# Attention outputs of the local heads: from a transposed product with moving probabilities to a row product with DMA transposes

## The chip, the core and the metric

The kernel runs on one core of one Trainium2 chip. The core has five engines that run side by side, each with its own queue of instructions taken in order: TensorE (PE, with its weight loads shown apart as PEld), VectorE (DVE), ScalarE (ACT), GpSimd (POOL) and SyncE (SP). SP issues DMAs and does no arithmetic. The metric is the device time of one execution in microseconds; lower is better.

## The reference

Two stages, float32 in and out.

```python
scores = scale * np.matmul(q, k.transpose(0, 1, 3, 2))        # (8, 8, 576, 576), head size 64
mask_local   = (rel >= 0) & (rel < 32)                        # heads 0 to 3
mask_strided = (rel >= 0) & (pos[None] % 32 == pos[:, None] % 32)   # heads 4 to 7
attn = softmax(np.where(masks, scores, -1e9))
attn_out = np.matmul(attn, v)
x = attn_out.transpose(0, 2, 1, 3).reshape(4608, 512)
out = (x @ w_a) * (x @ w_b) @ w_out                           # d_ff = 1536
```

`rel` is the query position minus the key position. A local head looks at the last 32 keys, a strided head at every 32nd key.

## The kernel before

**Stages.** The 4608 tokens are cut into nine FFN tiles of 512 tokens. A tile is 16 slots: slots 0 to 11 each compute one block of 128 of the 1536 hidden columns (`ffn_ab`: four matmuls of `wa_sb` and four of `wb_sb` against `xT`, L581, then the ACT copy L598 and the DVE product L601 or L603), and slots 12 to 15 compute the output of the tile (`ffn_y`, L768, for the tiles 0 and 1; `ffn_ys`, L686, for the others). A slot takes some 2 us. `xT` holds x transposed: 128 features on the partitions, four feature blocks `c` (two heads each), and room for four batches of 576 tokens. Tile b is the first that reads the tokens of batch b.

**Attention between the slots.** The attention of batch b is spread over the slots of tile b - 1. A batch is eight units u = 0 to 7: `c, half = u // 2, u % 2`. Units 0 to 3 are the local heads (c is 0 or 1, three blocks of 96 queries with windows of 128 keys), units 4 to 7 the strided heads. For each unit `S` makes the probabilities: score matmuls (L385), an ACT exponential into `p` (L393), a DVE mask (L403). One or two slots later `V` makes the outputs. The order is written out by hand: `LATER` puts V0, V1, V2, V3 of a batch after the slots 1, 3, 5, 7 of the tile and V4, V5, V6, V7 at 9, 11, 12.5 and 14, and `S0` of the next batch at -1, that is after slot 15. `STEPS` has the same for batches 1 and 2 at places of their own. After the steps of a slot come the entries of `at`, which hold loads, the DVE transposes `step_D` of the next batch's q and k, and the stores of the tile before. All engines take their instructions in this one order.

**Two forms of V.** Batches 0 and 1 use `V_p`, `V_r`, `V_n`: the probabilities are the weights and V with a column of ones moves through (L442, 65 columns), so that queries lie on the partitions and the row sum is one number per row; DVE takes a reciprocal (L450, of 96 x 6) and multiplies (L465, 96 x 384) into a tile `x` with queries on the partitions. `step_X` then transposes x on TensorE (L511) and copies it to `xT` on ACT (L523). Batches from `FIRST_D = 2` on use `step_VT`: V with 64 columns of ones is the weight and the probabilities move (L486, six matmuls of 96 columns for a local unit, eight of 72 for a strided one), so that the output is already transposed and the sums stand on the partitions 64 to 127. ACT takes the logarithm of the sums and the exponential of its negative (L495, L496) into a tile `r`, and two DVE products (L500 for local, L502 for strided units) write `xT`.

**Buffers.** `o`, the PSUM tile of V, has one buffer in this phase: the matmuls of a unit wait until the DVE products of the unit before have read it. The tile `x` of `V_n` (L458) and the tile `r` of `step_VT` (L488) have the same tag, `xr`, which has two buffers given in turn:

```python
x = sb.tile([128, RS * 4 * D], BF16, tag="xr", name="xr", bufs=2)                        # L458
r = sb.tile([128, RS * 4 * D], BF16, tag="xr", name="xr", bufs=2)[:64, :4 * W].bitcast(F32)  # L488
```

**SP's queue.** Each `step_D` ends in DMAs from SBUF to SBUF that SP issues (L342 two at a time for k, L346 four at a time for q). In the tile b - 1, where batch b's units run, the last part of b's own strided q is due at slot 1, which leads to ten DMAs in a row (qz four, kT two, qz four). From tile 2 on the stores of the tile before (`store_half`, L653, 512 KB each) are due at slots 2 and 3, from batch 3 on the last part of the local k of batch b + 1 at slot 5 (two DMAs) and that of its local q at slot 9 (ten more). For batch 3 itself, whose parts fall in tile 1, these two are due at slots 9 and 11 of that tile.

Of the kernel before, what the change touches and what calls it, by code (L numbers as in the profile page):

```python
# [14 lines left out]
FIRST_D = 2  # L15
# [6 lines left out]
LW = 96  # L22
# [8 lines left out]
def kernel(  # L31
# [10 lines left out]
    nc = tc.nc  # L42
    B, H, S, D = q.shape
# [114 lines left out]
    XR = 4  # L158
    xT = const.tile([128, KD, XR * S], BF16)
# [203 lines left out]
    def unit(u):  # L363

        c, half = u // 2, u % 2
        return (c, half, 128, LW, 3) if c < 2 else (c, half, NP, NP, 4)
# [46 lines left out]
    xn = {}  # L413

    def V_p(b, u):
        c, half, M, n, G = unit(u)
        p = ps.pop((b, u))
        if b == 0:

            o = psum4["o"].tile([128, 512], F32, tag="o", name="o")  # L420
            if c < 2:
                of = o[:, :2 * G * (D + 1)].rearrange("p (j g e) -> p j g e", j=2, e=D + 1)
                sm = of[:, :, :, D:]
            else:
                of = o.rearrange("p (j g e) -> p j g e", j=2, e=D)
                sm = psum4["sum"].tile([128, 2, 4, 1], F32, tag="sum", name="sum")
        else:
            o = psum4["o"].tile([128, 2, 512], F32, tag="o", name="o")
            of = o[:, :, :G * (D + 1)].rearrange("p j (g e) -> p j g e", e=D + 1)
            sm = of[:, :, :, D:]  # L430
        for i in range(G):
            for j in range(2):
                if c < 2:
                    vt = vl_buf[b % 2][:, (2 * c + j) * 6 + 3 * half + i, 0:D + 1]
                elif b == 0:
                    r = 2 * i + j
                    vt = nats[0, "v", c - 2][:NP, half, r * D:(r + 1) * D]
                else:
                    vt = vs_buf[b % 2][:, 2 * (c - 2) + half, 2 * i + j, 0:D + 1]
                w = vt.shape[1]  # L440
                pt = p[:M, j, i * n:i * n + 128]
                nc.tensor.matmul(of[:, j, i, :w], lhsT=pt, rhs=vt, start=True, stop=True)  # L442
                if b == 0 and c >= 2:
                    nc.tensor.matmul(sm[:, j, i], lhsT=pt, rhs=vl_buf[0][:M, 0, D:D + 1], start=True, stop=True)
        held[b, "o", u] = of[:n, :, :, :D], sm[:n]

    def V_r(b, u):
        c, half, M, n, G = unit(u)
        rc = sb.tile([128, 2, 4], F32, tag="rc", name="rc")
        nc.vector.reciprocal(rc[:n, :, :G].unsqueeze(3), held[b, "o", u][1])  # L450
        held[b, "rc", u] = rc

    def V_n(b, u):
        c, half, M, n, G = unit(u)
        ov, _ = held.pop((b, "o", u))
        rc = held.pop((b, "rc", u))
        if (b, c // 2) not in xn:
            x = sb.tile([128, RS * 4 * D], BF16, tag="xr", name="xr", bufs=2)  # L458
            xn[b, c // 2] = x[:n, :S // n * 4 * D].rearrange("p (g h d) -> p g h d", h=4, d=D)
        x = xn[b, c // 2][:, :, 2 * (c % 2):2 * (c % 2) + 2, :]  # L460
        if c < 2 or b >= FIRST_D:
            dst = x[:, G * half:G * half + G].rearrange("p g j d -> p j g d")
        else:
            dst = x[:, :, half, :].rearrange("p (g j) d -> p j g d", j=2)
        nc.vector.tensor_mul(dst, ov, rc[:n, :, :G].unsqueeze(3).to_broadcast([n, 2, G, D]))  # L465

    def step_V(b, u):
        if b >= FIRST_D:
            step_VT(b, u)
            return  # L470
        V_p(b, u)
        V_r(b, u)
        V_n(b, u)

    def step_VT(b, u):

        c, half, M, n, G = unit(u)
        p = ps.pop((b, u))
        o = psum4["o"].tile([128, 2, 512], F32, tag="o", name="o")
        for i in range(G):  # L480
            for j in range(2):
                if c < 2:
                    vt = vl_buf[b % 2][:, (2 * c + j) * 6 + 3 * half + i]
                else:
                    vt = vs_buf[b % 2][:, 2 * (c - 2) + j, 4 * half + i]
                nc.tensor.matmul(o[:, j, i * n:(i + 1) * n], lhsT=vt, rhs=p[:M, j, i * n:(i + 1) * n], start=True, stop=True)  # L486

        r = sb.tile([128, RS * 4 * D], BF16, tag="xr", name="xr", bufs=2)[:64, :4 * W].bitcast(F32)  # L488
        r = r.rearrange("p (j w) -> p j w", j=2)
        if c < 2:  # L490
            sums = o[64:, :, :W]
        else:

            sums, r = (t.rearrange(e, p=NP) for t, e in ((o[64:, :, :W], "d j (g p) -> d j p g"), (r, "d j (p g) -> d j p g")))
        nc.scalar.activation(r, sums, ACT.Ln)  # L495
        nc.scalar.activation(r, r, ACT.Exp, scale=-1.0)  # L496
        for j in range(2):
            dst = xT[64 * j:64 * j + 64, c, S * (b % XR):S * (b % XR + 1)]
            if c < 2:
                nc.vector.tensor_mul(dst[:, W * half:W * (half + 1)], o[:64, j, :W], r[:, j])  # L500
            else:
                nc.vector.tensor_mul(dst.rearrange("d (p r) -> d p r", r=RS)[:, :, G * half:G * (half + 1)],  # L502
                                     o[:64, j, :W].rearrange("d (g p) -> d p g", p=NP), r[:, j])
# [21 lines left out]
    def step_X(b, c):  # L525
# [20 lines left out]
    LATER = {-1: "S0", 0: "S1", 1: "V0", 2: "S2", 3: "V1", 4: "S3", 5: "V2", 6: "S4", 7: "V3", 8: "S5", 9: "V4", 10: "S6",  # L546
             11: "V5", 12: "S7", 12.5: "V6", 14: "V7"}
    FN = {"Tk": step_Tk, "Tq": step_Tq, "S": step_S, "V": step_V, "X": step_X, "W": lambda b, n: fast_w(n, slice(0, 3)),
          "s": S_px, "m": S_m, "L": lead_vl, "Pk": lambda b, c: pair_up("k", c), "Pq": lambda b, c: pair_up("q", c),
          "Z": lambda b, n: zero_qz(0, nc.vector, ((1, 1),)), "D": lambda b, n: step_D(FIRST_D, 0, "k", n)}  # L550
# [246 lines left out]
    with tc.manual_schedule(engines={ENG.PE, ENG.SP, ENG.Pool, ENG.DVE, ENG.Activation}):  # L797
# [11 lines left out]
        for x, src in ((raw[0], k), (raw[1], q)):  # L809
            nc.sync.dma_start(out=x[:96].rearrange("p (h r d) -> p h r d", h=2, d=D),  # L810
                              in_=src[0, 0:2].rearrange("h (p r) d -> p h r d", r=RL))
# [158 lines left out]
```

## Time and profile before

| what | value |
|---|---|
| time, median of 3 runs | 328.78 us (328.57 to 328.88) |
| span of the profiled execution, first to last instruction | 326.3 us |
| time of a run that lies outside such a span | 328.78 - 326.3 = 2.5 us |
| PE busy | 320.6 us, 98% of the span |
| DVE busy | 265.7 us, 81% |
| ACT busy | 202.7 us, 62% |
| POOL busy | 177.2 us, 54% |
| TensorE clock granted, mean | 0.999 |
| DMAs issued by SP for q and k (L342, L346), each | 0.59 us of SP's queue |

The profiled execution has a span and no time of its own; the 2.5 us are the difference between the median and that span. The tiles 1 to 6 take the stretches 57 to 92, 92 to 126, 126 to 160, 160 to 194, 194 to 228 and 228 to 262 us; batch b's units lie in tile b - 1.

How to read it: the page gives each engine's busy time, then the chain of work that ended last, then groups of instructions by source line with count, total, mean of one, and the idle time of the engine just before them with what ended it. The timeline gives single instructions with start and duration; a line with SPq is the issue of a DMA by SP, and its duration is how long SP's queue was held, not how long the data took.

### The profile page before, as it was taken

How to read it: one execution, taken by the hardware profiler on the slowest of the kernel's cores; microseconds unless marked ns; L12 is line 12 of the kernel's file. 1: busy time of each engine (PE TensorE's matmuls, PEld its weight loads, DVE VectorE, ACT ScalarE, POOL GpSimd, SP SyncE). 2: the span in 40 equal slices, each digit the busy share in tenths (PEclk: the TensorE clock that was granted, in tenths of full speed). 3: DMA queues.
4: the chain of work that ended last, by engine and by line, in shares of the span. 5: the costliest groups of instructions: out<-in, count | busy, mean ns of one | idle time of the engine just before them, and what ended most of it. 6: DMA issues, size and time to landing. Idle time of an engine off the chain costs nothing.

```text
span 326.3 us, 7676 instructions
## 1 busy us (share of the span) xinstructions
PE 320.6 (98%) x2820; PEld 205.5 (63%) x2820; DVE 265.7 (81%) x509; ACT 202.7 (62%) x329; POOL 177.2 (54%) x295
## 2 busy tenths in 40 slices
PE   8999999999999999999999999999999999999995
PEld 6754655455555587557999985569555954584474
DVE  6766888889778999999999999999877845647562
ACT  6764775478778765777677757875677643313321
POOL 8935839599966655875577557853312031232021
PEclk9999999999999999999999999999999999999999
DMA  9999999999999798799979999898033022004004
GB/s 151 154 204 201 204 184 182 173 171 136 132 213 116 95 97 79 77 217 125 83 72 199 138 86 77 160 180 84 20 77 115 2 67 64 0 2 129 1 2 129
DMA packets 98869, 37.50 MB, mean 115 GB/s; under 512 B 76688, under 2 KB 96016, under 8 KB 98832
## 3 DMA queue, kind: packets, MB, share of 16 engines
q0 software_dynamic: 85968, 19.48, 64.5%
q1 hardware_dynamic: 12576, 17.34, 18.4%
q8 instruction: 22, 0.36, 0.4%
q10 hardware_dynamic: 288, 0.20, 0.2%
q14 instruction: 15, 0.12, 0.1%
HBM read 39.51 MB, written 9.44 MB: 150 GB/s over the span
## 4 chain that ended last, share of the span: by engine, by line
PE 96%; DMA 2%; POOL 0%; DVE 0%; issue 0%; POOLq 0%; ACT 0%; DVEq 0%
PE mm L581 56%; PE mm L686 17%; PE mm L768 6%; PE st L385 5%; PE o L486 4%; DMA shared<-in_q_dram 2%; PE mm L714 2%; PE o L442 1%; PE ab L581 1%; PE misc L154 1%; PE tp L511 1%; PE tp L296 1%; PE end L714 1%; PE tp L287 0%; POOL shared L197 0%
## 5 line engine op out<-in xcount | busy, mean ns | idle before, releaser
L581 PE MATMUL mm<-xT,wa_sb 128*128 128x512 bf16 (+1 forms) x472 | 110.3, 357 | 0.0
L581 PE MATMUL mm<-xT,wb_sb 128*128 128x512 bf16 (+1 forms) x472 | 110.3, 357 | 0.0
L598 ACT COPY a_sb<-mm 128x512 f32<-128x512 f32 x106 | 62.1, 586 | 48.3 <-PE mm L581 47.6
L936 POOL CAST pace<-pf 1x1 f32<-1x1 bf16 x84 | 31.4, 374 | 84.0 <-DVE pf L601 80.7
L581 PEld LDWEIGHTS <-wb_sb 128*128 128x128 bf16 x480 | 46.3, 98 | 44.0 <-issue 0.2
L601 DVE TENSOR_TENSOR pf<-a_sb,mm 128x512 bf16<-128x512 f32 x84 | 56.4, 672 | 17.0 <-PE mm L581 13.8
L581 PEld LDWEIGHTS <-wa_sb 128*128 128x128 bf16 x480 | 42.7, 98 | 31.3
L393 ACT ACTIVATE p<-st 128x576 bf16<-128x576 f32 (+1 forms) x64 | 41.6, 650 | 11.7 <-PE st L385 11.1
L495 ACT ACTIVATE xr<-o 64x576 f32<-64x576 f32 x48 | 31.1, 649 | 25.0 <-PE o L486 24.2
L686 PEld LDWEIGHTS <-ps 128*128 128x128 bf16 x360 | 34.6, 98 | 3.9
L496 ACT ACTIVATE xr<-xr 64x576 f32<-64x576 f32 x48 | 32.9, 685 | 1.5
L500 DVE TENSOR_TENSOR xT<-o,xr 64x288 bf16<-64x288 f32 x48 | 21.5, 447 | 7.2 <-ACT xr L496 6.7
L502 DVE TENSOR_TENSOR xT<-o,xr 64x288 bf16<-64x288 f32 x48 | 21.5, 448 | 6.2 <-ACT xr L496 5.1
L686 PE MATMUL mm<-wf,ps 128*128 128x256 bf16 x216 | 26.4, 273 | 0.0
L768 PE MATMUL mm<-wo_sb,pf 128*128 128x512 bf16 x96 | 23.4, 379 | 0.0
L403 DVE TENSOR_TENSOR p<-p,mask_l 128x576 int16<-128x576 int16 x32 | 22.2, 694 | 1.2 <-ACT p L393 1.1
L243 POOL DMA_DIRECT2D vs<-in_v_dram x24 | 19.7, 821 | 3.0 <-PE st L385 2.2
L212 POOL DMA_DIRECT2D kl<-in_k_dram x24 | 16.1, 671 | 5.5 <-issue 3.6
L212 POOL DMA_DIRECT2D ql<-in_q_dram x24 | 16.0, 666 | 5.2 <-DMA wo_sb<-in_moe_w_out_dram 3.8
L603 DVE TENSOR_TENSOR pf<-a_sb,mm 128x512 bf16<-128x512 f32 x22 | 14.9, 676 | 4.3 <-ACT a_sb L598 2.8
L936 POOL COPY pace<-y_sb 1x1 f32<-1x1 f32 x16 | 2.8, 177 | 27.8 <-ACT y_sb L669 15.1
L686 PE MATMUL mm<-wf,pf 128*128 128x256 bf16 x144 | 17.6, 273 | 0.0
(162 smaller groups left out, 502.1 us busy)
## 6 DMA issues: line engine op xcount, KB each, us to landing
out_dram<-y_sb SPq DMA_DIRECT2D x12, 512.0 KB, 4.6
out_dram<-y_sb SPq DMA_DIRECT2D x10, 256.0 KB, 3.3
vl<-in_v_dram POOLq DMA_DIRECT2D x6, 384.0 KB, 6.8
kl<-in_k_dram POOLq DMA_DIRECT2D x24, 72.0 KB, 3.0
ql<-in_q_dram POOLq DMA_DIRECT2D x24, 72.0 KB, 3.0
vs<-in_v_dram POOLq DMA_DIRECT2D x24, 72.0 KB, 3.7
wo_sb<-in_moe_w_out_dram POOLq DMA_DIRECT2D x4, 384.0 KB, 9.2
natk<-in_k_dram POOLq DMA_DIRECT2D x20, 72.0 KB, 3.3
```

Of the source, the lines that this page charges most:

```text
L212: nc.gpsimd.dma_start(out=t[32 * h:32 * h + 32], in_=src[b, h].rearrange("(i y) d -> y i d", y=32))
L393: nc.scalar.activation(p[:M, :, :W], st[:M, :, :W], ACT.Exp, scale=scale)
L403: nc.vector.tensor_tensor(pi, pi, mk, op=ALU.bitwise_and)
L495: nc.scalar.activation(r, sums, ACT.Ln)
L496: nc.scalar.activation(r, r, ACT.Exp, scale=-1.0)
L500: nc.vector.tensor_mul(dst[:, W * half:W * (half + 1)], o[:64, j, :W], r[:, j])
L581: nc.tensor.matmul(ps_[:, c0:c0 + n], lhsT=w[:, kk, 128 * f:128 * (f + 1)], rhs=xT[:, kk, x0:x0 + n], start=(kk == first and c0 == 0), sto ...
L598: nc.scalar.copy(a_sb, ab[0])
L601: nc.vector.tensor_mul(pf[:, f, :].rearrange("p (i a s) -> p a i s", i=2, s=16), halves(a_sb), halves(ab[1]))
L686: nc.tensor.matmul(bank[b][:, q], lhsT=lhs(g, q), rhs=rhs(g), start=new and q == 0 and g == 0, stop=g == FG - 1, skip_group_check=True)
L768: nc.tensor.matmul(ybank[j], lhsT=pf[:, f, 128 * j:128 * (j + 1)], rhs=wo_sb[:, f], start=(f == 0), stop=(f == FD - 1))
L936: nc.gpsimd.tensor_copy(pace, done)
```

## The change

`step_V` sends the local units (c below 2) of batches 2 to 7 through `V_p`, `V_r` and `V_n`, as batches 0 and 1 do; strided units stay with `step_VT`. After the second half of each c, six DMA transposes, one per block of 96 queries, bring the block of x (96 queries x 128 features, bf16, 24 KB) into `xT`. SP issues them.

```diff
     def step_V(b, u):
-        if b >= FIRST_D:
+        c, half = u // 2, u % 2
+        if b >= FIRST_D and c >= 2:
             step_VT(b, u)
             return
         V_p(b, u)
         V_r(b, u)
         V_n(b, u)
+        if b >= FIRST_D and half == 1:
+            x = xn[b, 0]
+            for g in range(S // LW):
+                c0 = S * (b % XR) + LW * g
+                nc.sync.dma_start(out=xT[:, c, c0:c0 + LW],
+                                  in_=x[:, g, 2 * c:2 * c + 2].rearrange("p j d -> p (j d)"), transpose=True)
```

So each of six batches has four local units (24 in all) in the row form, and 12 DMA transposes (72 in all): six after V1 and six after V3. No instruction of the other units is changed, and no entry of the hand-written order.

## Prediction, made before the changed kernel was run

> **What bounds the kernel now.** I read the page's shares and its chain of work first.
>
> ```profile
> PE 320.6 (98%) x2820; PEld 205.5 (63%) x2820; DVE 265.7 (81%) x509; ACT 202.7 (62%) x329; POOL 177.2 (54%) x295
> PE 96%; DMA 2%; POOL 0%; DVE 0%; issue 0%; POOLq 0%; ACT 0%; DVEq 0%
> ```
>
> The chain is PE's for 96%. So only two things count: PE work that goes, and anything that makes PE wait. ACT and DVE work that goes is worth nothing by itself. Next the timeline around V5 of batch 5 (tile 4, a tile like most), all engines:
>
> ```profile
> 184.20 0.42 PE L486 MATMUL o<-p,vs 72*128 72x72 bf16 x8
> 184.66 0.65 ACT L495 ACTIVATE xr<-o 64x576 f32<-64x576 f32 x1 [0.55 <-PE o L486]
> 185.34 0.69 ACT L496 ACTIVATE xr<-xr 64x576 f32<-64x576 f32 x1
> 186.54 0.91 DVE L502 TENSOR_TENSOR xT<-o,xr 64x288 bf16<-64x288 f32 x2
> 188.22 0.43 PE L486 MATMUL o<-p,vs 72*128 72x72 bf16 x8
> ```
>
> V5's output leaves its only `o` buffer when L502 ends, at 187.45, and V6's matmuls take it at 188.22: 0.77 us of slack between an ACT instruction and PE. Then SP's queue in the same tile, the timeline of SP:
>
> ```profile
> 173.82 0.59 SPq L346 DMA_DIRECT2D qz10s<-tq  x1
> 174.45 0.60 SPq L346 DMA_DIRECT2D qz11s<-tq  x1
> 175.16 1.28 SPq L653 DMA_DIRECT2D out_dram<-y_sb  x2
> 176.55 3.33 SPq L342 DMA_DIRECT2D kT0l<-tk  x2
> 183.79 0.55 SPq L346 DMA_DIRECT2D qz00l<-tq  x1
> ```
>
> The reader is to see that SP is a real queue: a DMA from SBUF to SBUF holds it 0.59 us, and until 175.05 it is taken by ten of them whose first could start at 167.96. Behind two stores of 512 KB the next two took 3.33 us.
>
> **What the change does, part by part.**
>
> *PE, matmuls.* 24 units of six matmuls with 96 columns become six with 65. In the timeline a local unit of `step_VT` starts at 176.17 and the next matmul at 176.43: 0.26 us. A unit of L442 with 65 columns starts at 50.13 and its follower at 50.32: 0.19 us. 24 x 0.07 = 1.7 us less, on the path. That is all there is to gain.
>
> *ACT.* 24 x (649 + 685 ns) = 32 us go. Nobody waits for them now but the DVE products (ACT xr to DVE, 11.8 us of DVE idle in all), and DVE is not on the chain: 0.
>
> *DVE.* 24 x 2 x 447 ns = 21.5 us become 24 x (188 + 547 ns) = 17.6 us by the rows of L450 (96x6) and L465 (96x384). 3.9 us less, and V_n waits for PE alone, so `o` comes free earlier after a local unit. Hidden behind PE: 0.
>
> *PE, waits on DMAs.* `xT` now comes by 72 DMAs, so PE waits on DMA semaphores. A semaphore instruction at L486 takes 51 ns: 72 x 51 ns = 3.7 us at most, none if they pass while a matmul of 512 columns runs (eight take 1.73 us, 0.216 each). I take 0. The data itself has time: V3's transposes are due at slot 7 and the next tile reads at slot 16.
>
> *SP, 72 transposes.* The trace has none. SP is off the chain, so their cost lies in who waits for them. `x` and `r` share the tag `xr` with two buffers in turn: x of a batch takes one, r of V4 the other, and **r of V5 the one of x**. Its first writer is ACT's logarithm L495 of V5, and x is free only when the last of the 12 transposes has landed. Queued behind that logarithm on ACT are V5's exponential, the S7 exponential, the y copies; DVE's queue stands at L502; PE stands at V6, for `o`. The transposes of V3 in turn stand on SP behind everything due earlier. This wait is the heart of my forecast.
>
> *How long SP holds a transpose*, T, gap of 0.05 us included. Bounds: the shortest issue in SP's queue is 0.38 us (a store at 91.11), so 0.43; the longest SBUF-to-SBUF issue held behind stores is 2.13 us (143.97), so 2.18. I take **T = 0.9**: a plain DMA of this kind gives 0.64 and is the nearest row; the step up from it, for an operation of which no row tells, is my choice. Landing after issue: 1.8 to 3.7 us in these bursts, I take 3.0 (4.5 in tile 1, where the rows landed after 3.9 to 5.7).
>
> *Batch 5 worked out.* The burst of ten ends at 175.10. First store 0.7, six transposes 5.4, second store 0.7, the two of kT0l 1.3, the same hold behind the stores as now 2.1 (3.33 - 1.2), six transposes 5.4: SP ends at 190.7. The last was issued at 189.8 and lands at 192.8. V5's logarithm was at 184.66, so it starts 8.1 us late. Less the slack of 0.77, plus some 0.6 for V7 (L618, L403, L332, L616, L662 stand on DVE between V5's and V6's products, 3.3 us, and V7 follows V6 by 3.65 us with 0.2 us of slack): PE loses 7.9 us.
>
> *The other batches alike.* Batch 4: burst ends 140.57, hold 2.9, landed at 159.0, logarithm 150.40: 8.6 late, 8.5 lost. Batch 6: burst ends 208.56, hold 3.0, landed 227.1 against 218.69: 8.4 late, 8.3 lost. Batch 7: no local k behind the stores and loads over (DMA share 0.18 from 228 us on), so no hold and 2 us to land: 256.3 against 252.71, 3.6 late, 3.4 lost. Batch 3: burst ends 106.95, no such stores, 12 transposes and two kT: 121.1 against 116.37, 4.7 late, 4.6 lost. Batch 2: six transposes from 80.75 (behind kT1l), landed 89.8 against 85.04, 4.7 late, slack 0.34 there, 4.4 lost.
>
> Sum: 7.9 + 8.5 + 8.3 + 3.4 + 4.6 + 4.4 = **37.1 us lost**. Of the 1.7 us gained on PE I keep 0.4, what V0 saves (24 x 0.07 / 4): what comes later in a tile only lengthens the wait, since SP's burst sets when it ends. Net 36.7: the span goes from 326.3 to 363.0, and with the 2.5 us outside it, the time is **365.5 us**, against the median of 328.78.
>
> *What the unknowns move.* The sum changes by 11 T in five batches and 5 T in one, 60 us for each us of T. T = 0.43: 8.9 us, about 337. T = 0.64: 21.5 us, about 350. T = 2.18: 114 us, about 442. Each us of landing is worth 6 us, the hold behind the stores 8 us in all.
>
> *Two rules of the Trainium skill that stand against each other here.* "Advanced Engine Details and Errata", section "X-Bar Transpose (TRN2)", says that transposing DMAs are as fast as regular ones. "VectorE: DVE Perf Modes", section "The three transpose paths", gives 1309 ns for the DMA transpose of a 128 by 128 block against 390 ns on TensorE, and its table of rules sends a block to the DMA only where TensorE's PSUM output won't do, which speaks against this change. By the first the time would be about 350 us, as with the plain row of 0.64; by the second, read as 1.3 us of SP for each block, some 390 us. No run so far shows either.
>
> **The rivals.**
>
> *Faster: the transposes have landed when V5 asks.* Then only PE's 1.7 us remain: 327.1 us. This needs batch 5's last landing by 184.66 + 0.8. Without the transposes' own time the sum above reaches 179.9, plus 3.0 to land, and 11 T must fit in 2.6 us: T below 0.24, or a buffer of `xr` given otherwise than in turn. Against it: no issue in SP's queue is under 0.38. For it: landings near 1.8 us and no hold would allow 0.5. I give it 8%.
>
> *SP becomes the bound.* Now SP issues 24 DMAs and two stores in a tile of 34 us, 16.5 us. With T = 1.6 twelve more make 35.7: the local q of the next batch, due at slot 9 behind V3's transposes, comes late for S0 at slot 15 too. Time 37.1 + 60 x 0.7 = 79 us more, 408 us and up. For it: issues of 1.5 to 2.1 us behind stores. Against: most rows are at 0.59. 9%.
>
> *The DMA engines become the bound.* They are busy 95 to 98% in the stretches 92 to 228. Twelve transposes of 96 rows are 1152 packets a batch, at 39 ns (queue 0) to 76 ns (queue 1: 18.4% of 16 x 326.3 us over 12576 packets) over 16 engines 2.8 to 5.5 us. If the buffer wait is short and loads then miss their time, four tiles lose 11 to 22 us: 338 to 349 us. Against: DVE waited for a load 0.6 us in all. 7%.
>
> *Nothing to see*, the gain and a short wait cancelling: 2%.
>
> **How the numbers follow.** The buffer wait as worked out, with T between 0.43 and 1.6, has 74% and gives 336 to 410 us; its centre is my forecast, 365.5. The DMA rival lies inside. The range is 336 to 410; left out are the faster case, the cancelling one and the bound on SP, 19% together. Under 0.2% a measurement of this kernel can't be told from no change. Faster 0.08, within 0.2% 0.02, slower 0.90.
>
> **What would show it.** Right: ACT's L495 waits for the DMA `xT<-xr` six times, 3 to 9 us each, 38 us in all, at V5 alone; PE idles before L486 of V6, released by DVE L502; 72 DMAs of 24 KB on SP of some 0.85 us each; L495 and L496 fall to 24, L450 rises to 40; a local unit of L442 takes 0.19 us. Wrong: no wait of ACT on a DMA; waits of PE on the DMAs of `xT` at L581; DVE's V_n waiting for a transpose; idle PE at S0 instead of V6.

## The result, and the profile after

| what | before | after |
|---|---|---|
| time, median (lowest to highest) of 4 runs each | 328.83 us (328.57 to 328.94) | 396.98 us (396.13 to 399.35) |
| ratio, 95% interval | | 1.2064, 1.2 to 1.2128 |
| span of the profiled execution | 326.3 us | 394.5 us |
| PE busy | 320.6 us | 332.6 us, same 2820 matmuls |
| TensorE clock granted, mean | 0.999 | 0.922 |
| ACT busy | 202.7 us | 170.5 us |

The change makes the kernel slower by a fifth. The forecast was 365.5 us with a range of 336 to 410. Lines of the changed file stand 7 higher than before's from L474 on: the logarithm is now L502, the matmuls of the strided units L493, their products L509, the stores L660, the fast output L693. The transposes are issued at L479.

The page of the changed kernel: shares of the engines, the PE and clock rows of the 40 slices, the chain, and two groups.

```profile
PE 332.6 (84%) x2820; PEld 209.8 (53%) x2820; DVE 261.5 (66%) x509; ACT 170.5 (43%) x281; POOL 176.6 (45%) x295
PE   8999999991999399954999169990999739999995
PEclk9999999996899889995999869996799959999999
PE 69%; SPq 13%; DMA 6%; DVE 3%; ACT 3%; POOL 2%; issue 2%; POOLq 0%; ACTq 0%; DVEq 0%
L493 PE MATMUL o<-p,vs 72*128 72x72 bf16 x192 | 11.5, 209 | 55.5 <-DVE xT L509 55.5
L502 ACT ACTIVATE xr<-o 64x576 f32<-64x576 f32 x24 | 15.5, 647 | 74.5 <-DMA xT<-xr 55.8
```

The PE row has six holes, and the clock row has a dip at and after each. SP's queue, which was not in the chain before, has 13% of it, and the DMAs 6%. Of PE's 56.2 us of new idle time (394.5 - 332.6 against 326.3 - 320.6), 55.5 us stand ahead of one line, L493, and behind it stands a wait of ACT's logarithm on the DMA `xT<-xr`. The waits of that kernel (what waited, for what, us in all, times, longest):

```profile
PE o L493 <- DVE xT L509: 55.5, 6, 11.6
ACT xr L502 <- DMA xT<-xr: 55.8, 5, 13.4
ACT xr L502 <- DMA qz10l<-tq: 9.7, 1, 9.7
```

These are six waits of ACT, one in each of the batches 2 to 7: 9.75, 7.82, 11.06, 13.42, 12.87 and 10.58 us. One is put down to a q load; there too the logarithm began (95.05) 0.18 us after the last transpose had landed (94.87). The other five began 0.07 to 0.23 us after the last transpose of their batch. The timeline of tile 4 (V5 of batch 5) shows one of them; the last two lines come from its ACT and DVE queues, the first ones from PE's.

```profile
217.57 1.04 PE L693 MATMUL mm<-wf,ps 128*128 128x256 bf16 x8
230.21 0.64 PE L493 MATMUL o<-p,vs 72*128 72x72 bf16 x8 [11.61 <-DVE xT L509]
230.66 3.61 PE L693 MATMUL mm<-wf,ps 128*128 128x256 bf16 x16
...
227.76 0.65 ACT L502 ACTIVATE xr<-o 64x576 f32<-64x576 f32 x1 [13.42 <-DMA xT<-xr]
...
229.15 0.91 DVE L509 TENSOR_TENSOR xT<-o,xr 64x288 bf16<-64x288 f32 x2 [12.31 <-ACT xr L503]
```

ACT waits from 214.34 to 227.76, DVE's products follow, V6 on PE follows them. After that, sixteen matmuls of L693 take 3.61 us; in the kernel before sixteen of the same took 1.92:

```profile
188.48 1.92 PE L686 MATMUL mm<-wf,ps 128*128 128x256 bf16 x16
```

What the clock was can be read from busy times by stretch (length, busy us of PE, PEld, DVE, ACT and POOL, then granted clock, DMA share, GB/s):

```profile
218.60:223.90 5.30, 0.00 (x1) 0.00 (x0) 0.00 (x0) 0.00 (x0) 0.00 (x0) 1.00 0.73 82
223.90:230.20 6.30, 0.00 (x0) 0.02 (x1) 1.00 (x3) 2.38 (x4) 0.17 (x1) 0.50 0.15 35
230.20:234.10 3.90, 3.89 (x25) 2.92 (x26) 3.89 (x7) 1.41 (x3) 1.60 (x2) 0.50 0.81 101
234.10:238.70 4.60, 4.60 (x52) 4.14 (x51) 3.12 (x7) 2.50 (x4) 1.71 (x4) 1.00 0.24 22
```

The clock fell to 0.5 while PE stood, and stayed there for 3.9 us after PE had work again. The DMA engines were 73% busy in the first 5.3 us of the stall and 15% in the last 6.3, in which SP still issued transposes: there the queue that issues set the pace, not the transfers. SP's queue in the same tile:

```profile
204.38 0.59 SPq L346 DMA_DIRECT2D qz11s<-tq  x1
205.08 0.59 SPq L660 DMA_DIRECT2D out_dram<-y_sb  x1
205.71 9.41 SPq L479 DMA_TRANSPOSE xT<-xr  x6
215.23 0.59 SPq L660 DMA_DIRECT2D out_dram<-y_sb  x1
215.93 2.48 SPq L342 DMA_DIRECT2D kT0l<-tk  x2
218.46 8.08 SPq L479 DMA_TRANSPOSE xT<-xr  x6
226.66 0.56 SPq L346 DMA_DIRECT2D qz00l<-tq  x1
```

From the end of the burst of ten (204.97) to the end of the twelfth transpose (226.54) SP works without a gap. A transpose holds the queue 1.23 us (median of the 72), a plain DMA between SBUF places 0.59.

**Where the 68.2 us of span went.** 55.5 us are PE's six stalls (8.79, 6.01, 9.26, 11.61, 11.07, 8.78 us). 24.8 us of PE's busy time after them ran at half clock; half of that, 12.4 us, is my estimate of the loss. 1.8 us were gained: a local unit on PE takes 0.181 us where it took 0.255, 24 times. The sum is 66.1. Of the 2.1 us left, 0.95 arose before the change acts: the first output matmul of tile 0 started at 43.86 and not at 42.91. The rest is not assigned.

### The profile page after: what moved, and what is told of

Same layout as the page of the kernel before. It is cut to its first block, busy times and chain, and to the rows that moved or that the text cites. A ratio compares the mean times of both kernels' runs of the same rounds, so it can differ in the third digit from the quotient of the medians.

```text
span 394.5 us, 7706 instructions
## 1 busy us (share of the span) xinstructions
PE 332.6 (84%) x2820; PEld 209.8 (53%) x2820; DVE 261.5 (66%) x509; ACT 170.5 (43%) x281; POOL 176.6 (45%) x295
## 4 chain that ended last, share of the span: by engine, by line
PE 69%; SPq 13%; DMA 6%; DVE 3%; ACT 3%; POOL 2%; issue 2%; POOLq 0%; ACTq 0%; DVEq 0%
PE mm L588 42%; PE mm L693 13%; SPq L479 11%; PE mm L775 4%; DMA xT<-xr 3%; PE st L385 3%; SPq L342 2%; PE o L442 2%; PE o L493 2%; DMA vl<-in_v_dram 2%; DVE xT L509 2%; PE mm L721 1%; ACT xr L503 1%; ACT xr L502 1%; POOL shared L197 1%
## 5 line engine op out<-in xcount | busy, mean ns | idle before, releaser
L509 DVE TENSOR_TENSOR xT<-o,xr 64x288 bf16<-64x288 f32 x48 | 21.5, 448 | 77.5 <-ACT xr L503 77.1
L608 DVE TENSOR_TENSOR pf<-a_sb,mm 128x512 bf16<-128x512 f32 x84 | 56.5, 673 | 21.0 <-PE mm L588 17.6
L588 PEld LDWEIGHTS <-wa_sb 128*128 128x128 bf16 x480 | 42.3, 98 | 31.4
L493 PE MATMUL o<-p,vs 72*128 72x72 bf16 x192 | 11.5, 209 | 55.5 <-DVE xT L509 55.5
L502 ACT ACTIVATE xr<-o 64x576 f32<-64x576 f32 x24 | 15.5, 647 | 74.5 <-DMA xT<-xr 55.8
L693 PEld LDWEIGHTS <-ps 128*128 128x128 bf16 x360 | 39.4, 111 | 8.5
L493 PEld LDWEIGHTS <-vs 72*128 72x128 bf16 x192 | 10.0, 105 | 60.0 <-issue 57.2
L693 PE MATMUL mm<-wf,ps 128*128 128x256 bf16 x216 | 34.7, 326 | 0.0
L943 POOL COPY pace<-ya 1x1 f32<-1x1 f32 x6 | 2.0, 340 | 49.1 <-ACT ya L665 49.1
L465 DVE TENSOR_TENSOR xr<-o,rc 96x384 bf16<-96x384 f32 (+1 forms) x40 | 23.1, 579 | 1.3
L693 PE MATMUL mm<-wo_sb,ps 128*128 128x256 bf16 x144 | 18.7, 283 | 0.0
```

The costliest lines, as they stand in the source:

```text
L588: nc.tensor.matmul(ps_[:, c0:c0 + n], lhsT=w[:, kk, 128 * f:128 * (f + 1)], rhs=xT[:, kk, x0:x0 + n], start=(kk == first and c0 == 0), sto ...
L608: nc.vector.tensor_mul(pf[:, f, :].rearrange("p (i a s) -> p a i s", i=2, s=16), halves(a_sb), halves(ab[1]))
L693: nc.tensor.matmul(bank[b][:, q], lhsT=lhs(g, q), rhs=rhs(g), start=new and q == 0 and g == 0, stop=g == FG - 1, skip_group_check=True)
L943: nc.gpsimd.tensor_copy(pace, done)
```

## The experiments

Theory A, the prediction's: the tile `x`, which the transposes read, shares the tag `xr` with `r`, so V5's logarithm needs all twelve transposes landed, and SP's time for each of them sets when that is. Rival B: the stall has nothing to do with the buffer, and SP's time for the transposes would stop PE anyway, at S0, whose q loads queue behind them. A third question is whether SP's time goes by the instruction (A1) or by the block (A2).

### own: a buffer of its own for x

`x` of the batches from 2 on gets a tag of its own. The room for it comes from the V tiles of the local heads, cut from 128 to 80 columns a block, of which the row form reads 65.

```diff
+VL = 80
-    vl_buf = [const.tile([128, HL * 6, VW], BF16, name=f"vl{i}") for i in range(2)]
+    vl_buf = [const.tile([128, HL * 6, VL], BF16, name=f"vl{i}") for i in range(2)]
-            x = sb.tile([128, RS * 4 * D], BF16, tag="xr", name="xr", bufs=2)
+            x = sb.tile([128, RS * 4 * D], BF16, tag="xr", name="xr", bufs=2) if b < FIRST_D else sb.tile(
+                [128, RL * 4 * D], BF16, tag="xq", name="xq", bufs=1)
```

> The changed kernel with a buffer of its own for x (tag xq, one buffer), so that V5's r no longer waits for the transposes; the local V blocks take 80 columns instead of 128 to make room. Theory A (ACT's wait for x's buffer is the cause): the six waits of L495's counterpart on the DMA go, and with them the 55.5 us that PE stood before V6 and the 12 us of slower clock. But SP now needs 1.28 us for each transpose, so the local q of the next batch, behind V3's six, lands some 6 us after the place of S0 in the tiles 3, 4, 5 and some 3 us late in the tiles 1 and 2: PE idles at S0 instead, 25 us, time about 350 us (342 to 360). If SP has more room than that, 327 us. Theory B (SP or the DMA engines are the bound, whatever the buffer): 385 to 397 us, nearly unchanged.

Measured: 356.94 us (355.18 to 357.88), ratio to before 1.0839 (1.0778 to 1.0901); clock 0.971. ACT no longer waits for a DMA at the logarithm, and the 55.5 us at V6 are gone. PE's longest waits are now at the score matmuls:

```profile
PE st L386 <- DMA qz10l<-tq: 14.1, 3, 5.3
PE st L386 <- DMA qz00l<-tq: 4.5, 1, 4.5
```

SP's queue in tile 4 shows why:

```profile
203.87 7.79 SPq L481 DMA_TRANSPOSE xT<-xq  x6
211.77 0.67 SPq L347 DMA_DIRECT2D qz00l<-tq  x1
```

and PE's timeline has the wait:

```profile
215.25 0.20 PE L386 MATMUL st<-qz00l,kT0l 128*128 128x96 bf16 x1 [4.50 <-DMA qz00l<-tq]
```

The local q of the next batch, due at slot 9, is issued only from 211.77 on, behind V3's six transposes, and S0 stands 4.50 us for it, until 215.25. Five such stalls (tiles 1 to 5: 4.22, 1.1, 5.33, 4.5 and 4.57 us) make 19.7 us, and PE's busy time is 7.4 us above before's, at a clock that was 0.5 for 20.5 us. So the buffer is what the changed kernel waits for, and a buffer of its own is worth 396.98 - 356.94 = 40 us. Behind it stands the stall at S0 that B names, which the first one had hidden; with it the time is still 28 us above before's. Of B, only that stall is borne out: that the buffer has nothing to do with it, and the 385 to 397 us, are refuted.

### xr3: a third buffer for the shared tag

```diff
-            x = sb.tile([128, RS * 4 * D], BF16, tag="xr", name="xr", bufs=2)
+            x = sb.tile([128, RS * 4 * D], BF16, tag="xr", name="xr", bufs=3)
-        r = sb.tile([128, RS * 4 * D], BF16, tag="xr", name="xr", bufs=2)[:64, :4 * W].bitcast(F32)
+        r = sb.tile([128, RS * 4 * D], BF16, tag="xr", name="xr", bufs=3)[:64, :4 * W].bitcast(F32)
```

(with the same cut of the V tiles.)

> The changed kernel with three buffers for the tag xr instead of two (and local V blocks of 80 columns to make room). In turn, x's buffer then goes to r of V6 and not of V5, whose logarithm is due 4.0 us later (3.1 in tile 1). Theory A: each of the six waits moves from V5 to V6 and PE's from V6 to V7, and each gets some 4 us shorter: 55.5 us of PE idle become about 32, and with shorter idle times the clock drops less: 366 to 374 us. Theory B (SP's load itself): unchanged, 395 to 398 us.

Measured: 377.79 us (375.23 to 380.43), ratio 1.148 (1.1397 to 1.1562); clock 0.946. The waits, to be held against those of the changed kernel:

```profile
PE o L494 <- DVE xT L510: 37.5, 6, 8.3
ACT xr L503 <- DMA xT<-xr: 47.3, 6, 10.1
```

The same six waits are there, each one unit later: with three buffers in turn it is V6 that gets x's, and PE idles before V7. One unit more of time saves 18 us of the 55.5. The direction is A's; the size was missed, 37.5 us of idle PE where about 32 were expected, and the clock was 0.5 for 41.0 us, so that the time lies above the interval expected. The edit changes the buffers' turn and the width of the V tiles, and own has the same width without the wait: it is the turn that moved it by one unit.

### one: a single transpose for the six blocks of a pair of heads

`x` is laid out with the feature block c outermost, so that one DMA instruction can take all six blocks of 96 x 128; 12 instructions in place of 72. The buffers are the change's.

```diff
+                xn[b, 0] = x[:n, :RL * 4 * D].rearrange("p (c g j d) -> p g c j d", c=2, j=2, d=D)
...
-            for g in range(S // LW):
-                c0 = S * (b % XR) + LW * g
-                nc.sync.dma_start(out=xT[:, c, c0:c0 + LW],
-                                  in_=x[:, g, 2 * c:2 * c + 2].rearrange("p j d -> p (j d)"), transpose=True)
+            c0 = S * (b % XR)
+            nc.sync.dma_start(out=xT[:, c, c0:c0 + S].rearrange("p (g n) -> p g n", n=LW),
+                              in_=x[:, :, c].rearrange("p g j d -> p (g j d)"), transpose=True)
```

> The changed kernel with xr as it was (two buffers), but x laid out with c outermost, so that one DMA transpose brings all six blocks of a c (96 rows by 768 columns): 12 transposes in place of 72, the same bytes. Theory A1 (SP holds 1.23 us for each instruction, whatever its size): SP is free 6.4 us earlier after each group, V5 no longer waits: 327 to 332 us. Theory A2 (SP holds 0.2 us for each tile of 16 rows): one instruction holds it 7.4 us, the wait stays: 390 to 398 us. The rival that DMA engines bind: no gain either, but with short issues in SP's queue and long landings.

Measured: 339.21, 343.64 and 343.65 us (a fourth run, 346.31, does not enter the ratio), ratio 1.0374 (1.0264 to 1.0485). Neither number was met, but the question is answered: SP is held 1.20 to 1.45 us by an instruction of six blocks where no store stands directly ahead, as by one of a single block. SP's queue in tile 3 (batch 4):

```profile
139.46 0.61 SPq L662 DMA_DIRECT2D out_dram<-y_sb  x1
140.18 2.71 SPq L481 DMA_TRANSPOSE xT<-xr  x1
142.99 0.87 SPq L662 DMA_DIRECT2D out_dram<-y_sb  x1
143.96 3.02 SPq L342 DMA_DIRECT2D kT1l<-tk  x2
147.07 1.45 SPq L481 DMA_TRANSPOSE xT<-xr  x1
```

What A1 left out is what the stores ahead do: SP holds the first transpose and the two kT1l behind them longer (2.71 and 3.02 us), and the landing is late. The transpose issued at 147.07 landed 7.67 us later, behind two stores of 512 KB, and ACT's line of that tile reads

```profile
154.85 0.65 ACT L504 ACTIVATE xr<-o 64x576 f32<-64x576 f32 x1 [4.63 <-DMA qz11l<-tq]
```

(the load it names ended close by; the transpose landed at 154.75). Three long waits are left, in the batches 4, 5 and 6: 4.63, 6.05 and 5.18 us, with landings of 7.67, 6.33 and 5.13. PE idles 10.4 us for them, and the clock was 0.5 for 3.4 us around each, in 9.4 us of PE's busy time. The run of 339.21 us, whose mean clock was 0.999, suggests what that costs: it is 4.4 us shorter. These are the batches in which both stores of 512 KB and a load of local k stand ahead of the second transpose. Batches 2 and 3 have no such stores; batch 7 has them, but no local k, so that its second transpose was issued 4.4 us after the burst of ten ended (261.14 - 256.76) and not 7.7 (147.07 - 139.35). The batches 3 and 7 wait for no DMA; in batch 2 ACT waits 1.60 us (the transpose landed at 86.02, 5.06 us after its issue), which costs PE 0.65 us.

### own_one: both at once

> Both: x in a buffer of its own and one transpose for each c. Theory A1: nothing waits, PE's 1.7 us remain as the gain: 327 us. Theory A2: SP as full as with 72 transposes, PE idles at S0, about 350 us, as in the run with the own buffer alone.

Measured: 327.31 us (326.94 to 330.26, 10 runs) against 328.46, ratio 0.9967 (0.9938 to 0.9996); span 325.4. The page's first line is that of the kernel before, less 1.1 us:

```profile
PE 319.5 (98%) x2820; PEld 204.0 (63%) x2820; DVE 259.8 (80%) x509; ACT 171.0 (53%) x281; POOL 174.4 (54%) x295
```

No gap of PE above 0.8 us is left in the stretch of the change. With 12 instructions on SP and no compute instruction waiting for their landing, both mechanisms are gone, and what stays fits PE's shorter local units. The cut of the V tiles is in this kernel too; no run has it alone, so its part in the gain, if any, isn't told apart.

### tr_alone: the transposes alone, nobody waiting for them

The kernel before, with 72 transposes of a constant added where the change has them. They write a part of `xT` that is written again before it is read: work that the kernel doesn't need.

```diff
         if b >= FIRST_D:
             step_VT(b, u)
+            c, half = u // 2, u % 2
+            if c < 2 and half == 1:
+                for g in range(S // LW):
+                    c0 = S * ((b + 1) % XR) + LW * g
+                    nc.sync.dma_start(out=xT[:, c, c0:c0 + LW], in_=ident[:LW], transpose=True)
             return
```

> The kernel before, all units in its own form, with 72 DMA transposes of 96 x 128 added at the places of the change; they read the identity and write a part of xT that is written again before anyone reads it, so no unit waits for them. What is told apart: SP's time for the transposes by itself. Theory A: the local q of the next batch stands behind them on SP and PE idles at S0, as in the run with the own buffer (20 us of idle, 10 us of half clock); without that run's shorter local units about 358 us (350 to 362). If 72 transposes on SP cost nothing without the buffer wait: 328 to 330 us.

Measured: 363.94 us (359.08 to 364.04), ratio 1.1022 (1.0948 to 1.1096), a little above what was expected. Of the profiled run (364.04 us), 4.6 us were lost before the first added transpose (issued at 78.4): PE waited 1.60 us for a load of V at the start, its clock was 0.5 from 17.96 to 24.78, and the first output matmul came at 47.56 where before has 42.91. The waits:

```profile
PE st L385 <- DMA qz10l<-tq: 12.9, 3, 5.1
PE st L385 <- DMA qz00l<-tq: 7.9, 2, 5.0
```

The five stalls at S0 (20.8 us) stand in the same five tiles as own's (19.7 us). No data is waited for that a transpose brings, no buffer is shared: SP's queue time by itself costs some 30 us in this kernel (359.08 - 328.80 in the fastest run; 362.3 - 326.3 - 4.6 = 31.4 in the profiled one). This is the prediction's rival "SP becomes the bound", and it needs no buffer.

### one_late: the landing taken away instead of the shared buffer

As `one`, with the two stores of a tile moved behind V3's transpose.

```diff
-                do(16 * t + 18, store_half, 0)
+                do(16 * t + 24, store_half, 0)
...
-                do(16 * t + 19, store_half, 1)
+                do(16 * t + 25, store_half, 1)
```

> One transpose for each c and the two buffers of xr, as in the run that had 343.65 us, and the stores of a tile issued six slots later (slots 8 and 9 of the next tile), behind V3's transpose and not ahead of it. Theory: what is left of the wait there (three waits of ACT in the tiles 3 to 5, where the transpose landed 7.7 us after its issue behind two stores of 512 KB) is the landing behind the stores. Then V5 no longer waits and the time is 327 to 330 us. If the landing is long by itself (36 blocks in one transpose), the waits stay: 341 to 346 us.

Measured: 328.84 us (327.94 to 332.04, 10 runs) against 328.8, ratio 1.0 (0.9971 to 1.003). The three waits are gone, as expected. The stores ahead had delayed the second transposes twice: in the batches 4 to 6 these are now issued 3.8 to 4.7 us after the burst of ten (7.7 to 9.6 in `one`), and land after 2.7 to 4.7 us (5.1 to 7.7). The expectation had named the landing alone; the earlier issue is the larger part in two of the three. In batch 2 a wait of 0.91 us stays. The 1.8 us of PE's shorter units do not show. The late store holds its `y` buffer longer, and PE meets that:

```profile
PE mm L590 <- ACT y_sb L678: 0.7, 2, 0.4
```

That is 0.7 us; the rest of the missing gain wasn't found.

### own_one_r: own_one once more, in five rounds

> The version with a buffer of its own for x and one transpose for each c, again, with more rounds: 24 local units of 0.181 us in place of 0.255 us are 1.8 us less; 326.9 to 327.3 us against 328.5, a ratio of 0.995 to 0.997.

Measured: 327.19 us (326.74 to 327.95, 11 runs) against 328.8 (21 runs), ratio 0.9946 (0.9924 to 0.9967). This version is faster than both kernels, by half a per cent, about 1.6 us. Its PE timeline has the local unit at 0.19 us (start of the first line to start of the next):

```profile
107.73 0.35 PE L443 MATMUL o<-vl,p 128*128 128x65 bf16 x6
107.92 1.02 PE L592 MATMUL mm<-xT,wa_sb 128*128 128x512 bf16 x4
```

## Why the prediction was right, and where its sum was short

**Right: the mechanism.** The wait is where the prediction put it: ACT's logarithm of V5, in each of the six batches, on the DMA `xT<-xr`; PE before V6, released by the DVE product. own and xr3 show that it is the shared tag's turn: a buffer of its own removes the wait, a third buffer moves it by one unit. The size was short: six waits of 3 to 9 us, 38 in all, were named, and they were 7.8 to 13.4 us, 65.5 in all; the span grew by 68.2 us where 36.7 were forecast.

**Mis-sized: T, SP's time for a transpose.** Taken as 0.9 us, measured 1.23 + 0.05 = 1.28, and that put the time at 365.5 + 22.8 = 388.3 us. The prediction's own rule of 60 us for each us of T makes 22.8 us of it, and 37.1 + 22.8 = 59.9 us against 55.5 measured: one term corrected, the idle time is there within 8%. Its bounds of 0.43 and 2.18 held it (the lower one was misread: the shortest issue in SP's queue before is 0.33 us, a store at 54.16, not 0.38). The choice near the plain DMA's 0.64 was the weak step: a different operation had no row, and the middle of the bounds, 1.3, would have been nearer here.

**Missing: the clock.** After each of the six stalls PE came back at half speed. Some 12.4 us of the 68.2 are lost that way and no term of the sum had them; that the range still held the time is owed to its reach up to T = 1.6. The two clock rows above show it directly. The Trainium skill states the rule on its page "TensorE: Matmul & The Clock Gate", section "Why this matters for your kernels": no idle gaps of TensorE over about 3 us between bursts of matmuls, or the clock falls back to half. The runs here agree roughly, and the edge isn't sharp: a gap of 1.10 us (own) kept the clock, gaps of 2.76 (tr_alone) and 2.83 us (`one`) lost it, one of 2.92 us (tr_alone) kept it, and all from 3.38 us on lost it.

**Smaller terms.** The last landing took 2.2 to 2.4 us where 3.0 was taken (-0.6 us a batch), 5.28 in tile 1 where 4.5 was taken. The hold behind the stores was 2.5 to 3.6 us where 2.1 to 3.0 was taken; batch 7 had some 2.3 us of it where none was taken, which is part of why it lost 8.8 us and not 3.4 + 11 x 0.38 = 7.6. In batch 2 the second six had to wait for the first six, still on SP until 81.81. PE's gain was 1.8 us by the length of the units (1.7 taken); how much of it outlived the stalls (0.4 taken) is too small to be seen beside them.

**The rivals.** *Faster* needed T below 0.24 and fell; its 327.1 us is what own_one measures (327.31, and 327.19 in own_one_r), once neither wait is there. *SP becomes the bound* was given from T = 1.6 on, reckoned by the tile's 34 us against SP's 16.5 us plus 12 T. That left out the hold behind the stores: 16.5 + 12 x 1.28 + 3.1 = 35.0 us, already over. tr_alone and own show its stall at T = 1.28. It isn't load alone: between two stalls of own (174.76 to 215.25, 40.5 us) SP still idled 3.0 us, before the strided q, and what stalls S0 is that its q is issued after V3's transposes. In the changed kernel PE has no wait for a q at L385; the likely reason is that the first wait holds up the whole tile, and with it S0. *The DMA engines* did not bind: they were 73%, then 15% busy in the stall, and the run `one`, which moves the same bytes in 12 instructions, took 53 us less.

**The two rules weighed.** By the rule that transposing DMAs are as fast as regular ones the sum gave some 350 us, by the 1309 ns some 390. Measured is 1.23 us of SP against 0.59 for a plain DMA, and 396.98 us: the second was nearer. But 1.23 us is a price of the issue and not of the block: one instruction with six blocks held SP 1.20 to 1.45 us. The median landing was 3.3 us with one block.

## What to carry to other kernels

Where a DMA reads a tile, its buffer is taken until the DMA has landed: look for who gets that buffer next in turn, because that instruction waits for the whole queue ahead of the DMA, and everything behind it on its engine waits too. Price a DMA on its issuing queue by the instruction and put many blocks into one, and look at what large stores ahead of it do to its issue and its landing. When a stall of PE is forecast at several us, add what the clock costs afterwards, here 2 us each, and ask what is late next once the stall is cured.

## What the runs showed of the hardware

- A DMA transpose of a 96 x 128 bf16 block from SBUF to SBUF held SP's queue 1.23 us (lowest 1.09), one of six such blocks 1.20 to 1.45, a plain DMA from SBUF to SBUF 0.59.
- Directly behind a store of 512 KB on the same queue an issue was held longer (2.7 to 3.5 us for a six-block transpose). Behind two of them the second transposes of the batches 4 to 7 landed after 4.5 to 7.7 us (`one`); with the stores after them, 2.5 to 4.7 (one_late).
- In the changed kernel the clock of PE stood at 0.5 for 6.8, 10.2 or 13.7 us around stalls of 6.0 to 11.6 us, steps of 3.4 us. It fell 2.1 to 5.3 us after the stall had begun and came back 3.5 to 4.9 us after PE had work again. Stalls of 2.8 to 5.3 us in own, `one` and tr_alone brought 3.4 or 6.8 us at 0.5, or none (2.92 us in tr_alone).
